# Two kinds of matmuls into one PSUM bank, in alternation or in separate runs

## The chip, the cores and the metric

The kernel runs on one NeuronCore of a Trainium2 chip. The metric is the device time of one execution in microseconds (us), median of several runs. The engines are named as in the profile: PE is TensorE's matmul, PEld its weight load, DVE is VectorE, ACT ScalarE, POOL GpSimd, SP SyncE (here it issues transfers only).

## What is computed

Three blocks follow one another; the change is in the first, a recurrent attention over 768 positions, 4 x 8 heads of 40 elements:

```python
for t in range(S):
    kt, vt, rt = (k[:, :, t], v[:, :, t], r[:, :, t])
    wt, at, bt = (w[:, :, t], a[:, :, t], b[:, :, t])
    y[:, :, t] = np.einsum('bhd,bhde->bhe', rt, state)
    Sa = np.einsum('bhde,bhe->bhd', state, at)
    state_decay = state * wt[:, :, None, :] - np.einsum('bhd,bhe->bhde', Sa, bt)
    state = state_decay + np.einsum('bhd,bhe->bhde', vt, kt)
# then, on x = y with the heads side by side, [4, 768, 320]:
#   u = x + real(fft over positions and features); x = u + relu(norm(u) @ w_ch1) @ w_ch2
#   u = x + token mixing (w_tok1, w_tok2);         x = u + relu(u @ w_ch1) @ w_ch2
```

## The kernel before, in words

**Attention in chunks.** The 768 positions are cut into 12 steps `i` of L=64 positions, each of two halves `c` of H=32. The 32 heads, padded to 33, stand in NG=11 groups `g` of three (3 x 40 = 120 partitions). What the names in the rows mean, in the order of one step: `load` and `decay` bring in and scale the inputs (`bt`, `a`, `R`), `kg` multiplies keys (tile `RT`), `inv` and `merge` make from that a small inverse per head (through `Ge`, `Me`, `Ad` in DRAM, then `AT`, `Mq`, the products mg and mc, tile `Mst`), `kbts` and `pts` transpose (`kbt`, `PT`). Then `chain` carries the state through the two halves: product x (from `L0T` or `L1T`), copied by ScalarE to `X`; product z, copied by ScalarE to `VZt`; product s, added by VectorE into the next half's `L1T` or `L0T`. This is the only part in which a step waits for the step before.

**The outputs of a step: `outp`.** st and zt transpose the state (`SS`, one tile for each half) and `VZt` (`Zd`). For three pairs `k2` of groups of heads, sc multiplies queries (`rm`) with `Zd` and `Vd`, and VectorE masks the result (line 525, tile `sc`). Then y is summed in PSUM from two products for each head, group and half: line 536 multiplies `rm` with the state `SS` (120 rows, 32 columns of the array), line 537 adds the masked `sc` times `kbt` (64 rows from 64c, 32 columns). The result of half c of the x-th group lies on partitions 64x+32c to 64x+32c+31, 40 columns wide; four such quadrants and up to 12 column blocks fill one bank. The groups k=0 to 3 use the bank first, then k=4 and 5; there is one bank for this (`BANKS` has 'y': 1). At the end VectorE multiplies the bank by `PT` into `ys` (line 550; in the last step into `X`, line 543), and that frees the bank.

In step 0 the state before the first half is zero, so line 536 runs only for c=1. That makes 759 products of line 536 and 792 of line 537.

**What sets the order.** Nothing is ordered by hand. Every operation is put into a plan with an engine, a cost, the tiles that it reads and writes and the banks that it takes and frees (`P.op`). `Plan.emit` then walks through a modelled time and gives each engine the ready operation with the earliest latest-start time; `SLACK`, `PW`, `HOLDBACK` and the table `OFF` (a shift for each stage and step) enter into that choice. Where the modelled TensorE has little to do, fillers are laid in (`warm`, 128 x 128 products of the identity). The engines run their lists in that order, whatever the real durations are. The plan charges one y product 0.0275 us (`.33*m` for 12 products of each of m groups).

**After attention.** `begin` frees attention's memory and loads `W1`, `W2` for the first dense block (products hps and acc); the FFT is done with psA and mix; weights are split into high and low parts on VectorE, ScalarE and GpSimd (`job`, tiles `mdraw`, `mdt`, `mda`, `mdh`) beside that.

Of the kernel before, what the change touches and what calls it, by code (L numbers as in the profile page):

```python
# [191 lines left out]
class Attn:  # L192
# [305 lines left out]
    def outp(s,i):  # L498
# [16 lines left out]
        for k2 in range(3):  # L515
            ks=[k for k in (2*k2,2*k2+1)]; gl=[g for k in ks for g in ((k,k+6) if k<5 else (k,))]; m=len(gl); j=(3*i+k2)%NSB; t=s.sc[j]
            hs=s.psum('m',[128,512],"sc"); kc=('ps',hs[0])
            def f(gl=gl,hs=hs):
                ps=s.pst(hs)
                for x,g in enumerate(gl):  # L520
                    for z in range(2):
                        for c in range(2):
                            q=64*c+32*z; nc.tensor.matmul(ps[q:q+32,96*x:96*x+96],lhsT=ZV[z][:,g,H*c:H*c+H],rhs=rm[:,:,g,H*c:H*c+H],start=True,stop=True,skip_group_check=True)  # L523
            P.op('PE',.175*m,f,[('Zd',c) for c in range(2)]+['Vd']+[('rm',p,x) for x in range(3)],[kc,('sc',j)],alloc=hs[0],cols=720*m)
            P.op('DVE',.06+.104*m,lambda t=t,m=m,hs=hs: nc.vector.tensor_tensor(out=t[:,:3*m],in0=s.pst(hs)[:,:96*m].rearrange("p (n t) -> p n t",t=H),in1=s.tri.unsqueeze(1).to_broadcast([128,3*m,H]),op=ALU.mult),[kc,'tri'],[('sc',j)],free=[hs[0]])  # L525
            for k in ks:
                gs=(k,k+6) if k<5 else (k,); m=len(gs)
                if k%4==0:
                    k0=k; hy=s.psum(YB,[128,512],"y"); ky=('ps',hy[0])
                def f(k=k,gs=gs,t=t,hy=hy,k0=k0,gl=gl):  # L530
                    ps=s.pst(hy); c0=120*(k-k0)
                    for hh in range(3):
                        for x,g in enumerate(gs):
# [4 lines left out]
                P.op('PE',.33*m,f,[('rm',p,x) for x in range(3)]+['PT']+[('SS',c) for c in range(0 if i else 1,2)]+[('sc',j),('kbt',i%2)]+([ky+(k0,)] if k>k0 else []),[ky+(k,),('ys',k0)],alloc=hy[0] if k==k0 else None,cols=550*m)
                if i==NSC-1:
                    def mul(u,c,n,hy=hy,k0=k0):  # L540
                        def f(u=u,c=c,n=n,hy=hy,k0=k0):
                            o=s.X[64:128,NSC//2-1].rearrange("p b f -> p (b f)")[:,720*u+c:720*u+c+n]; q=slice(64*u,64*u+64)
                            nc.vector.tensor_tensor(out=o,in0=s.pst(hy)[q,c-120*k0:c-120*k0+n],in1=s.PT[q,c:c+n],op=ALU.mult)
                        P.op('DVE',.06+n*.00106,f,[ky+(y,) for y in range(k0,k+1)]+['PT','close'],[s.xkey(NSC//2-1,('X',i,u,c),720*u+c,n)],free=[hy[0]])
                    if k==2: mul(0,0,360)
                    if k==3: mul(0,360,120); mul(1,0,480)
                    if k==5: mul(0,480,240); mul(1,480,80)
                elif k%4==3 or k==5:
                    def mul(p,c,n,hy=hy,k0=k0):
                        P.op('DVE',.06+n*.00106,lambda: nc.vector.tensor_tensor(out=s.ys[:p,c:c+n],in0=s.pst(hy)[:p,c-120*k0:c-120*k0+n],in1=s.PT[:p,c:c+n],op=ALU.mult),[ky+(y,) for y in range(k0,k+1)]+['PT'],[('ys',k0)],free=[hy[0]])  # L550
                    if k==3: mul(128,0,480)
                    else: mul(128,480,120); mul(64,600,120)
# [98 lines left out]
OFF={'chain': -1.1, 'dec2': 32.2, 'decay': -11.2, 'decode': 1174.5, 'fft': -18.4, 'fft2': -1420.0, 'inv': 0.7, 'kbts': -133.0, 'kg': 2.6, 'load': 73.5,
     'load2': 68.0, 'load3': 495.9, 'loada': 131.7, 'merge': 3.4, 'mlp': 7.2, 'out_tile': -9569.3, 'outp': -0.2, 'pad': 3861.2, 'pts': 110.3,
     'tok': -129.6, 'tok2': -4363.1, 'wdec': 1.9, ('chain', 0): 2.8, ('chain', 1): -0.6, ('chain', 10): -27.7, ('chain', 11): -1181.9,
     ('chain', 2): 2.4, ('chain', 3): 3.1, ('chain', 4): -28.8, ('chain', 5): 1.6, ('chain', 6): 10.0, ('chain', 7): -6253.9, ('chain', 8): -6.2,
     ('chain', 9): -251.5, ('dec2', 0): 39.5, ('decay', 0): -3367.0, ('decay', 1): -9097.8, ('decay', 10): 806.6, ('decay', 11): 4028.4,
     ('decay', 2): -7768.2, ('decay', 3): -4130.3, ('decay', 4): -433.7, ('decay', 5): 3269.8, ('decay', 6): -1157.5, ('decay', 7): 39.5,
     ('decay', 8): -61.1, ('decay', 9): 6.7, ('decode', 0): 1792.1, ('fft', 0): 35.6, ('fft', 1): -29.7, ('fft', 2): -87.9, ('fft', 3): -3601.5,
     ('fft2', 0): 1089.4, ('fft2', 1): -4113.9, ('fft2', 2): -6989.6, ('fft2', 3): 1198.8, ('inv', 0): -4891.5, ('inv', 1): 31.7, ('inv', 2): -3.2,
     ('inv', 3): -25.1, ('inv', 4): -0.6, ('inv', 5): -2644.4, ('inv', 6): -32.2, ('kbts', 0): -5730.2, ('kbts', 1): -4115.9, ('kbts', 10): -4321.1,
     ('kbts', 11): -5664.7, ('kbts', 2): -8815.0, ('kbts', 3): 105.3, ('kbts', 4): -3543.6, ('kbts', 5): 3004.9, ('kbts', 6): -571.5,  # L660
     ('kbts', 7): -4566.8, ('kbts', 8): -1632.3, ('kbts', 9): -4092.9, ('kg', 0): -290.4, ('kg', 1): -112.1, ('kg', 10): -27.7, ('kg', 11): -10105.2,
     ('kg', 2): -1226.0, ('kg', 3): -3903.3, ('kg', 4): -41.2, ('kg', 5): -4.3, ('kg', 6): -8.6, ('kg', 7): 31.3, ('kg', 8): -81.7,
     ('kg', 9): 1517.4, ('load', 0): -9400.7, ('load', 1): -7102.3, ('load', 10): -126.6, ('load', 11): 2473.4, ('load', 2): -251.0,
     ('load', 3): -59.8, ('load', 4): -55.0, ('load', 5): -56.4, ('load', 6): -422.8, ('load', 7): -102.7, ('load', 8): 833.6, ('load', 9): 1196.8,
# [4 lines left out]
     ('loada', 0): -8412.4, ('loada', 1): -306.7, ('loada', 10): 354.9, ('loada', 11): 3605.4, ('loada', 2): -1343.5, ('loada', 3): -2356.9,  # L669
     ('loada', 4): -100.1, ('loada', 5): 2846.4, ('loada', 6): 2227.9, ('loada', 7): 1032.9, ('loada', 8): 2713.4, ('loada', 9): -197.4,  # L670
     ('merge', 0): -4614.6, ('merge', 1): -5007.5, ('merge', 10): 66.6, ('merge', 11): 19.4, ('merge', 2): 1.1, ('merge', 3): -993.9,
     ('merge', 4): 1021.8, ('merge', 5): -653.9, ('merge', 6): -0.8, ('merge', 7): -10626.2, ('merge', 8): 4254.3, ('merge', 9): 46.5,
     ('mlp', 0): -91.8, ('mlp', 1): -0.1, ('mlp', 2): 27.3, ('mlp', 3): 38.4, ('out_tile', None): 5521.2, ('outp', 0): -3.2, ('outp', 1): 5.8,
     ('outp', 10): 2.3, ('outp', 11): -1451.3, ('outp', 2): 0.3, ('outp', 3): -14.1, ('outp', 4): -1.2, ('outp', 5): 2.6, ('outp', 6): -51.3,
     ('outp', 7): -1.8, ('outp', 8): 1.3, ('outp', 9): 57.3, ('pad', 0): -12666.1, ('pts', 0): 1883.5, ('pts', 1): -5413.7, ('pts', 10): -1354.5,
     ('pts', 11): -2249.8, ('pts', 2): -129.1, ('pts', 3): -687.3, ('pts', 4): 1669.8, ('pts', 5): -3554.0, ('pts', 6): -3523.7, ('pts', 7): -115.1,
# [457 lines left out]
```

## Time and profile before

| | us |
|---|---|
| median of 3 runs | 1414.76 (1413.27 to 1424.5) |
| profiled execution | 1415.79 |
| its span, first to last instruction | 1414.1 |
| PE busy | 1358.7 (96%) |
| PEld busy | 1185.6 (84%) |
| DVE busy | 598.8 (42%) |
| ACT busy | 369.9 (26%) |
| POOL busy | 245.0 (17%) |

Busy times are of the whole span. How late a stage begins, at which granted clock TensorE works in it and what it waits for there is read from windows and from the chain of waits. The granted clock is given as a share of 2.4 GHz; it has two levels, 1.00 (2.4 GHz) and 0.50 (1.2 GHz), and a number between them is a mean over time.

### The profile page before, as it was taken

How to read it: one execution, taken by the hardware profiler on the slowest of the kernel's cores; microseconds unless marked ns; L12 is line 12 of the kernel's file. 1: busy time of each engine (PE TensorE's matmuls, PEld its weight loads, DVE VectorE, ACT ScalarE, POOL GpSimd, SP SyncE). 2: the span in 40 equal slices, each digit the busy share in tenths (PEclk: the TensorE clock that was granted, in tenths of full speed). 3: DMA queues.
4: the chain of work that ended last, by engine and by line, in shares of the span. 5: the costliest groups of instructions: out<-in, count | busy, mean ns of one | idle time of the engine just before them, and what ended most of it. 6: DMA issues, size and time to landing. Idle time of an engine off the chain costs nothing.

```text
span 1414.1 us, 36859 instructions
## 1 busy us (share of the span) xinstructions
PE 1358.7 (96%) x16271; PEld 1185.6 (84%) x16271; DVE 598.8 (42%) x1340; ACT 369.9 (26%) x818; POOL 245.0 (17%) x346
## 2 busy tenths in 40 slices
PE   6479999999999999989999999999999999999999
PEld 5467777877777777767877799999999999999998
DVE  5664331435333332110321397877772732323222
ACT  3342131423223222130211142332331411212121
POOL 8530112212120201010011120333442000000000
PEclk9675565666565665555555699999999999999999
DMA  8874222527242231270113231334449000000000
GB/s 180 143 143 108 60 59 44 119 60 150 68 122 70 64 77 47 48 207 16 50 49 103 103 132 62 112 120 138 135 153 335 1 1 15 15 15 15 14 15 28
DMA packets 140478, 120.01 MB, mean 85 GB/s; under 512 B 97983, under 2 KB 117951, under 8 KB 140191
## 3 DMA queue, kind: packets, MB, share of 16 engines
q1 hardware_dynamic: 135519, 94.00, 26.8%
q0 software_dynamic: 4800, 23.67, 4.8%
q8 instruction: 127, 2.08, 0.6%
q14 instruction: 32, 0.26, 0.1%
HBM read 82.26 MB, written 30.61 MB: 80 GB/s over the span
## 4 chain that ended last, share of the span: by engine, by line
PE 88%; DMA 4%; DVE 3%; issue 2%; POOL 1%; ACT 1%; SPq 1%; ACTq 0%; POOLq 0%; DVEq 0%
PE hps L962 17%; PE acc L952 16%; PE y L537 14%; PE y L536 14%; PE s L481 3%; PE sc L523 3%; PE kg L322 2%; PE z L467 2%; PE kbt L429 2%; PE x L460 2%; PE st L505 2%; PE zt L512 2%; PE psA L869 2%; PE mix L896 1%; PE tps L1026 1%
## 5 line engine op out<-in xcount | busy, mean ns | idle before, releaser
L537 PE MATMUL y<-kbt,sc 64*32 64x40 f32 x1584 | 247.3, 258 | 0.0
L536 PE MATMUL y<-SS,rm 120*32 120x40 f32 x1518 | 246.3, 259 | 0.6 <-issue 0.6
L965 DVE SCALAR_TENSOR_TENSOR hl<-hps,hh 128x384 fp32r<-128x384 f32 x176 | 97.9, 557 | 230.2 <-ACT hh L964 230.0
L537 PEld LDWEIGHTS y<-kbt,sc 64*32 64x32 f32 x1584 | 130.7, 132 | 64.1 <-issue 0.8
L536 PEld LDWEIGHTS y<-SS,rm 120*32 120x32 f32 x1518 | 131.5, 133 | 61.5 <-PE warm L54 0.2
L964 ACT ACTIVATE hh<-hps 128x384 fp32r<-128x384 f32 x176 | 86.4, 491 | 328.1 <-PE hps L962 328.1
L962 PE MATMUL hps<-th,v 128*128 128x384 f32 x576 | 142.4, 338 | 0.0
L952 PE MATMUL acc<-v,hh 128*128 128x320 f32 x576 | 129.0, 311 | 0.0
L962 PE MATMUL hps<-th,W 128*128 128x384 f32 x480 | 120.1, 338 | 1.0 <-DVE hl L965 1.0
L952 PE MATMUL acc<-W,hh 128*128 128x320 f32 x480 | 107.6, 311 | 0.0
L962 PEld LDWEIGHTS hps<-th,v 128*128 128x128 f32 x576 | 103.7, 188 | 0.0
L952 PEld LDWEIGHTS acc<-v,hh 128*128 128x128 f32 x576 | 97.9, 188 | 0.0
L550 DVE TENSOR_TENSOR ys<-y,PT 128x480 f32<-128x480 f32 (+2 forms) x33 | 13.0, 403 | 191.4 <-PE y L537 178.4
L57 POOL TENSOR_SCALAR_AFFINE_SELECT RT<-RT 32x384 f32<-32x384 f32 (+1 forms) x66 | 43.7, 670 | 267.7 <-ACT RT L236 265.6
L952 PE MATMUL acc<-v,hl 128*128 128x320 f32 x288 | 89.1, 309 | 0.0
L962 PEld LDWEIGHTS hps<-th,W 128*128 128x128 f32 x480 | 86.8, 188 | 1.4 <-DVE hl L965 1.3
L830 POOL TENSOR_TENSOR mda<-mda,mdh 128x320 f32<-128x320 f32 (+2 forms) x44 | 45.0, 1027 | 208.5 <-ACT mdh L827 94.8
L952 PEld LDWEIGHTS acc<-W,hh 128*128 128x128 f32 x480 | 81.0, 188 | 0.0
L952 PE MATMUL acc<-W,hl 128*128 128x320 f32 x240 | 74.1, 309 | 0.6 <-DVE hl L965 0.6
L525 DVE TENSOR_TENSOR sc<-sc,tri 128x384 f32<-128x384 f32 (+1 forms) x36 | 18.7, 523 | 111.8 <-PE sc L523 111.5
L962 PE MATMUL hps<-tl,v 128*128 128x384 f32 x192 | 64.6, 337 | 0.0
L236 ACT ACTIVATE VZt<-z 32x320 f32<-32x320 f32 x96 | 41.0, 428 | 70.9 <-PE z L467 69.1
(190 smaller groups left out, 2279.7 us busy)
## 6 DMA issues: line engine op xcount, KB each, us to landing
bt<-in_bkR_dram SPq DMA_DIRECT2D x12, 660.0 KB
mdraw<-in_moe_w_ch_dram SPq DMA_DIRECT2D x22, 320.0 KB
wS<-in_wR_dram SPq DMA_DIRECT2D x12, 335.2 KB
a<-in_aR_dram SPq DMA_DIRECT2D x12, 335.2 KB
Vd<-in_vR_dram SPq DMA_DIRECT2D x12, 330.0 KB
VZt<-in_vT_dram SPq DMA_DIRECT2D x24, 165.0 KB
rm<-in_rR_dram SPq DMA_DIRECT2D x36, 110.0 KB
out_dram<-ou SPq DMA_DIRECT2D x24, 160.0 KB
```

What stands on the lines that cost most here:

```text
L57: nc.gpsimd.affine_select(out=o,in_=o,pattern=pattern,compare_op=ALU.is_gt,fill=0.0,base=base,channel_multiplier=-1)
L236: s.P.op('ACT',cost,lambda: s.nc.scalar.activation(out=out,in_=in_() if callable(in_) else in_,func=AF.Copy,**k),R,W,free=free,due=due)
L322: for c in range(2): nc.tensor.matmul(ps[64*c:64*c+64,96*y:96*y+96],lhsT=bt[:,g+y,c].rearrange("p v t -> p (v t)"),rhs=am[:,:,g+y,H*c:H*c+ ...
L481: for v in range(2): n=2*w+v+4*x; nc.tensor.matmul(ps[64*v:64*v+40,x],lhsT=s.kbt[p][64*c:64*c+64,n],rhs=VZt[64*c:64*c+64,n],start=True,sto ...
L523: q=64*c+32*z; nc.tensor.matmul(ps[q:q+32,96*x:96*x+96],lhsT=ZV[z][:,g,H*c:H*c+H],rhs=rm[:,:,g,H*c:H*c+H],start=True,stop=True,skip_group_ ...
L536: if i or c: nc.tensor.matmul(o,lhsT=rm[:,hh,g,H*c:H*c+H],rhs=s.SS[c][:,g],start=True,stop=False,skip_group_check=True)
L537: nc.tensor.matmul(o,lhsT=t[64*c:64*c+64,3*gl.index(g)+hh],rhs=kbt[64*c:64*c+64,3*g+hh],start=i==0 and c==0,stop=True,skip_group_check=True)
L830: P.op('POOL',.07+d*.00237,lambda: nc.gpsimd.tensor_tensor(out=g("da").bitcast(F32),in0=g("da").bitcast(F32),in1=g("dh").bitcast(F32),op=A ...
L952: nc.tensor.matmul(s.pst(acc[x]),lhsT=a[:,sl],rhs=t[w2][w][:,m],start=(m==0 and n==0),stop=(m==MT-1 and n==2))
L962: for n,(l,r) in enumerate(ops): nc.tensor.matmul(ps,lhsT=l,rhs=r,start=n==0,stop=n==7)
L964: s.act(384,lambda: nc.scalar.activation(out=t["hh"][z],in_=s.pst(h),func=AF.Relu),[kp],[('hh',z)],free=[h[0]])
L965: s.dve(.47,lambda: nc.vector.scalar_tensor_tensor(out=t["hl"][z],in0=s.pst(h),scalar=0.0,in1=t["hh"][z].bitcast(F32),op0=ALU.max,op1=ALU. ...
```

## The change

In `outp` the two products are no longer issued one behind the other. For each use of the bank, first all products with the state go in one operation of the plan (line 525 of the changed kernel: all k of the bank, 48 or 18 products, in step 0 24 or 9), ahead of the sc products; then, as each masked `sc` tile is there, the products with `kbt` go in one operation (line 544; 24 or 18). A product carries the clearing flag (`start`) only where its quadrant has not been begun in this use of the bank (`begun`); before, each product of line 536 cleared. The plan charges the same 0.0275 us for a product. The number and the shapes of all products are the same. The multiplications by `PT` are the same in steps 0 to 10; in the last step the first two are one. `SLACK`, `PW`, `HOLDBACK` and `OFF` have other numbers.

```diff
-SLACK=4.21018271644813
+SLACK=2.103090933238401
...
-            for k in ks:
-                gs=(k,k+6) if k<5 else (k,); m=len(gs)
-                if k%4==0:
-                    k0=k; hy=s.psum(YB,[128,512],"y"); ky=('ps',hy[0])
-                def f(k=k,gs=gs,t=t,hy=hy,k0=k0,gl=gl):
-                    ps=s.pst(hy); c0=120*(k-k0)
+        gk=lambda k: (k,k+6) if k<5 else (k,)
+        bank={}
+        for k0,kr in ((0,range(4)),(4,range(4,6))):
+            hy=s.psum(YB,[128,512],"y"); ky=('ps',hy[0]); begun=set(); bank[k0]=(hy,ky,begun); n=sum(len(gk(k)) for k in kr)
+            def f(hy=hy,k0=k0,kr=kr,begun=begun):
+                ps=s.pst(hy)
+                for k in kr:
                     for hh in range(3):
-                        for x,g in enumerate(gs):
+                        for x,g in enumerate(gk(k)):
+                            for c in range(0 if i else 1,2):
+                                q=64*x+H*c; o=120*(k-k0)+40*hh; nc.tensor.matmul(ps[q:q+H,o:o+40],lhsT=rm[:,hh,g,H*c:H*c+H],rhs=s.SS[c][:,g],start=q not in begun,stop=False,skip_group_check=True); begun.add(q)
+            P.op('PE',.165*n,f,[('rm',p,x) for x in range(3)]+[('SS',c) for c in range(0 if i else 1,2)],[ky,('ys',k0)],alloc=hy[0],cols=275*n)
...
-                                q=64*x+H*c; o=ps[q:q+H,c0+40*hh:c0+40*hh+40]
-                                if i or c: nc.tensor.matmul(o,lhsT=rm[:,hh,g,H*c:H*c+H],rhs=s.SS[c][:,g],start=True,stop=False,skip_group_check=True)
-                                nc.tensor.matmul(o,lhsT=t[64*c:64*c+64,3*gl.index(g)+hh],rhs=kbt[64*c:64*c+64,3*g+hh],start=i==0 and c==0,stop=True,skip_group_check=True)
...
+                def f(ks=ks,gl=gl,t=t,hy=hy,k0=k0,begun=begun):
+                    ps=s.pst(hy)
+                    for k in ks:
+                        for hh in range(3):
+                            for x,g in enumerate(gk(k)):
+                                for c in range(2):
+                                    q=64*x+H*c; o=120*(k-k0)+40*hh; nc.tensor.matmul(ps[q:q+H,o:o+40],lhsT=t[64*c:64*c+64,3*gl.index(g)+hh],rhs=kbt[64*c:64*c+64,3*g+hh],start=q not in begun,stop=True,skip_group_check=True); begun.add(q)
+                P.op('PE',.165*m,f,['PT',('sc',j),('kbt',i%2),ky]+([ky+(0,)] if k2==1 else []),[ky+(k2,)],cols=275*m)
...
-PW=2680.8127923252287
-HOLDBACK=63.60602034250026
+PW=7653.7623164983115
+HOLDBACK=0.0
```

TensorE's list of the kernel before, at the start of the y products of step 1 (the names carry tile numbers: SS_155 and SS_156 are the states of the two halves, rm_142 the queries, sc_159 the masked tile):

```order
L523 MATMUL sc<-rm_142,Zd_143 32x96 x2
L523 MATMUL sc<-rm_142,Vd_144 32x96 x2
L481 MATMUL s<-VZt_140,kbt_152 40x40 x16
L536 MATMUL y<-SS_155,rm_142 32x40
L537 MATMUL y<-kbt_153,sc_159 32x40
L536 MATMUL y<-SS_156,rm_142 32x40
L537 MATMUL y<-kbt_153,sc_159 32x40
```

The last four rows repeat through the step: every product with the state is followed by one with `kbt`.

TensorE's list of the changed kernel, in step 2's chain (x, z and s there), behind the first part of step 1's y products:

```order
L467 MATMUL z<-X_145,Mst_146 32x40 x32
L544 MATMUL y<-kbt_153,sc_158 32x40 x24
L512 MATMUL zt<-ident,VZt_140 120x32 x11
L481 MATMUL s<-VZt_140,kbt_152 40x40 x32
L525 MATMUL y<-SS_155,rm_142 32x40
L525 MATMUL y<-SS_156,rm_142 32x40
```

Line 544 stands in a run of 24 between two links of the chain; line 525 begins a run of 18 (one row each, since the two halves read different tiles).

TensorE's list of the changed kernel, in step 0 (where only one half has products with the state) and the chain around it:

```order
L460 MATMUL x<-L1T_138,RT_132 32x40 x32
L505 MATMUL st<-ident,L1T_138 120x40 x11
L467 MATMUL z<-X_145,Mst_146 32x40 x32
L322 MATMUL kg<-am_117,bt_123 64x96 x6
L525 MATMUL y<-SS_156,rm_141 32x40 x24
L481 MATMUL s<-VZt_140,kbt_152 40x40 x32
L512 MATMUL zt<-ident,VZt_140 120x32 x11
```

The run with the state has moved ahead of step 0's sc products, between z and s of the same step, where no y product stood before.

## Rows read from the trace of the kernel before

**Rows 1.** Windows of three stretches: us; busy PE, PEld, DVE, ACT, POOL; PEclk, DMA, GB/s

```profile
0.00:100.00 100.00, 62.57 (x1364) 55.56 (x1364) 59.10 (x101) 41.10 (x77) 63.90 (x111) 0.79 0.84 162
100.00:802.00 702.00, 691.16 (x10966) 527.95 (x10967) 215.68 (x464) 163.14 (x355) 89.09 (x129) 0.58 0.31 77
802.00:1415.00 613.00, 605.02 (x3943) 602.12 (x3941) 324.01 (x777) 165.66 (x386) 92.01 (x106) 1.00 0.25 81
```

**Rows 2.** Window of the long stretch, PE, instructions of the tile y alone

```profile
100.00:802.00 702.00, 390.01 (x3102) 0.58 0.31 77
```

**Rows 3.** The page's cost groups of the two y products

```profile
L537 PE MATMUL y<-kbt,sc 64*32 64x40 f32 x1584 | 247.3, 258 | 0.0
L536 PE MATMUL y<-SS,rm 120*32 120x40 f32 x1518 | 246.3, 259 | 0.6 <-issue 0.6
```

**Rows 4.** Timeline of PE, step 1, clock 0.50: start, us, instructions

```profile
155.56 0.34 PE L536 MATMUL y<-SS,rm 120*32 120x40 f32 x2
155.83 0.34 PE L537 MATMUL y<-kbt,sc 64*32 64x40 f32 x2
```

**Rows 5.** Timeline of PE around 213 us, clock 1.00

```profile
213.02 0.26 PE L536 MATMUL y<-SS,rm 120*32 120x40 f32 x2
213.21 0.26 PE L537 MATMUL y<-kbt,sc 64*32 64x40 f32 x2
```

**Rows 6.** Timeline of PE, step 0, clock 0.50

```profile
102.71 0.35 PE L537 MATMUL y<-kbt,sc 64*32 64x40 f32 x4
102.98 0.34 PE L536 MATMUL y<-SS,rm 120*32 120x40 f32 x2
```

**Rows 7.** The chain of waits at clock 0.50: start, us, what

```profile
110.54 2.29 PE s L481 x64
...
117.48 1.22 PE x L460 x64
...
147.84 1.22 PE z L467 x64
...
298.87 2.86 PE warm L54 x12
```

**Rows 8.** The chain of waits from 256 to 262 us, at the higher clock

```profile
256.11 0.72 PE z L467 x64
...
259.92 1.35 PE s L481 x64
```

**Rows 9.** The page's cost group of the reader of the y bank

```profile
L550 DVE TENSOR_TENSOR ys<-y,PT 128x480 f32<-128x480 f32 (+2 forms) x33 | 13.0, 403 | 191.4 <-PE y L537 178.4
```

**Rows 10.** Windows free of y, first to last of ten, and sum (columns as rows 1)

```profile
70.00:100.00 30.00, 22.91 (x717) 20.31 (x709) 18.48 (x33) 14.46 (x29) 12.59 (x20) 0.84 0.80 165
130.00:155.50 25.50, 25.50 (x546) 21.25 (x546) 14.17 (x25) 9.06 (x19) 5.41 (x8) 0.50 0.44 103
...
250.00:270.00 20.00, 20.00 (x429) 17.39 (x432) 12.31 (x23) 13.84 (x28) 8.95 (x13) 0.70 0.67 155
320.00:330.00 10.00, 9.97 (x193) 8.74 (x195) 6.82 (x15) 5.07 (x12) 2.14 (x2) 0.82 0.85 147
...
690.00:710.00 20.00, 19.87 (x663) 17.24 (x665) 15.83 (x33) 8.61 (x24) 4.34 (x4) 0.52 0.22 66
sum 175.50, PE 162.68 PEld 139.48 DVE 99.11 ACT 80.44 POOL 39.80; mean PE 16.27 PEld 13.95 DVE 9.91 ACT 8.04 POOL 3.98
```

**Rows 11.** The chain of waits, the longest DMA of the merge

```profile
614.83 9.62 DMA Mq<-Me
```

**Rows 12.** The chain of waits from the last y product to the first hps

```profile
801.08 0.28 PE y L537 x2
...
804.70 8.11 DMA W<-m10h
...
835.92 2.82 PE hps L962 x16
```

More of the change, by code (lines that the diff above doesn't have):

```diff
@@ L514, in outp @@
             s.act(.4,s.Zd[:,:,H*c:H*c+H],lambda hz=hz: s.pst(hz)[:120,:H*NG].rearrange("p (g t) -> p g t",t=H),[kz],[('Zd',c)],free=[hz[0]])
[L515 to L525, printed above, removed]
-            for k in ks:
-                gs=(k,k+6) if k<5 else (k,); m=len(gs)
-                if k%4==0:
-                    k0=k; hy=s.psum(YB,[128,512],"y"); ky=('ps',hy[0])
-                def f(k=k,gs=gs,t=t,hy=hy,k0=k0,gl=gl):
-                    ps=s.pst(hy); c0=120*(k-k0)
-                    for hh in range(3):
-                        for x,g in enumerate(gs):
-                            for c in range(2):
-                                q=64*x+H*c; o=ps[q:q+H,c0+40*hh:c0+40*hh+40]
-                                if i or c: nc.tensor.matmul(o,lhsT=rm[:,hh,g,H*c:H*c+H],rhs=s.SS[c][:,g],start=True,stop=False,skip_group_check=True)
-                                nc.tensor.matmul(o,lhsT=t[64*c:64*c+64,3*gl.index(g)+hh],rhs=kbt[64*c:64*c+64,3*g+hh],start=i==0 and c==0,stop=True,skip_group_check=True)
[L538 to L552, printed above, removed]
@@ new lines, in outp, with f, mul @@
+        gk=lambda k: (k,k+6) if k<5 else (k,)
[5 more added lines that the diff above has]
+                for k in kr:
+                    for hh in range(3):
+                        for x,g in enumerate(gk(k)):
+                            for c in range(0 if i else 1,2):
+                                q=64*x+H*c; o=120*(k-k0)+40*hh; nc.tensor.matmul(ps[q:q+H,o:o+40],lhsT=rm[:,hh,g,H*c:H*c+H],rhs=s.SS[c][:,g],start=q not in begun,stop=False,skip_group_check=True); begun.add(q)
+            P.op('PE',.165*n,f,[('rm',p,x) for x in range(3)]+[('SS',c) for c in range(0 if i else 1,2)],[ky,('ys',k0)],alloc=hy[0],cols=275*n)
+            for k2 in ((0,1) if k0==0 else (2,)):
+                ks=(2*k2,2*k2+1); gl=[g for k in ks for g in gk(k)]; m=len(gl); j=(3*i+k2)%NSB; t=s.sc[j]
+                hs=s.psum('m',[128,512],"sc"); kc=('ps',hs[0])
+                def f(gl=gl,hs=hs):
+                    ps=s.pst(hs)
+                    for x,g in enumerate(gl):
+                        for z in range(2):
+                            for c in range(2):
+                                q=64*c+32*z; nc.tensor.matmul(ps[q:q+32,96*x:96*x+96],lhsT=ZV[z][:,g,H*c:H*c+H],rhs=rm[:,:,g,H*c:H*c+H],start=True,stop=True,skip_group_check=True)
+                P.op('PE',.175*m,f,[('Zd',c) for c in range(2)]+['Vd']+[('rm',p,x) for x in range(3)],[kc,('sc',j)],alloc=hs[0],cols=720*m)
+                P.op('DVE',.06+.104*m,lambda t=t,m=m,hs=hs: nc.vector.tensor_tensor(out=t[:,:3*m],in0=s.pst(hs)[:,:96*m].rearrange("p (n t) -> p n t",t=H),in1=s.tri.unsqueeze(1).to_broadcast([128,3*m,H]),op=ALU.mult),[kc,'tri'],[('sc',j)],free=[hs[0]])
+                def f(ks=ks,gl=gl,t=t,hy=hy,k0=k0,begun=begun):
[6 more added lines that the diff above has]
+                P.op('PE',.165*m,f,['PT',('sc',j),('kbt',i%2),ky]+([ky+(0,)] if k2==1 else []),[ky+(k2,)],cols=275*m)
+            rd=[ky+(k2,) for k2 in ((0,1) if k0==0 else (2,))]+['PT']
+            if i==NSC-1:
+                def mul(u,c,n,hy=hy,k0=k0,rd=rd):
+                    def f(u=u,c=c,n=n,hy=hy,k0=k0):
+                        o=s.X[64:128,NSC//2-1].rearrange("p b f -> p (b f)")[:,720*u+c:720*u+c+n]; q=slice(64*u,64*u+64)
+                        nc.vector.tensor_tensor(out=o,in0=s.pst(hy)[q,c-120*k0:c-120*k0+n],in1=s.PT[q,c:c+n],op=ALU.mult)
+                    P.op('DVE',.06+n*.00106,f,rd+['close'],[s.xkey(NSC//2-1,('X',i,u,c),720*u+c,n)],free=[hy[0]])
+                if k0==0: mul(0,0,480); mul(1,0,480)
+                else: mul(0,480,240); mul(1,480,80)
+            else:
+                def mul(p,c,n,hy=hy,k0=k0,rd=rd):
+                    P.op('DVE',.06+n*.00106,lambda: nc.vector.tensor_tensor(out=s.ys[:p,c:c+n],in0=s.pst(hy)[:p,c-120*k0:c-120*k0+n],in1=s.PT[:p,c:c+n],op=ALU.mult),rd,[('ys',k0)],free=[hy[0]])
+                if k0==0: mul(128,0,480)
+                else: mul(128,480,120); mul(64,600,120)
@@ L647 @@
 DD=60
-PW=2680.8127923252287
-HOLDBACK=63.60602034250026
+PW=7653.7623164983115
+HOLDBACK=0.0
 RING=128
[L651 to L664, printed above, removed]
[4 rows of a table removed]
[L669 to L676, printed above, removed]
-     ('pts', 8): 181.0, ('pts', 9): -66.1, ('tok', 0): -5025.5, ('tok', 1): 26.2, ('tok', 2): -3238.5, ('tok', 3): -8655.9, ('tok2', 0): -1545.8,
-     ('tok2', 1): -6681.6, ('tok2', 2): -6326.6, ('tok2', 3): 2095.9, ('wdec', 0): -11.4}
@@ new lines @@
+OFF={'chain': -0.6, 'dec2': 135.9, 'decay': -912.9, 'decode': -748.7, 'fft': -2.8, 'fft2': -2475.1, 'inv': 0.2, 'kbts': 1.2, 'kg': 2.7, 'load': 2.2,
+     'load2': 25.3, 'load3': 117.9, 'loada': 74.1, 'merge': -2.6, 'mlp': -975.6, 'out_tile': 6704.8, 'outp': -0.2, 'pad': 2438.9, 'pts': -0.7,
+     'tok': 3296.0, 'tok2': -2095.0, 'wdec': 10.9, ('chain', 0): -3181.0, ('chain', 1): 0.1, ('chain', 10): -4853.9, ('chain', 11): -878.4,
+     ('chain', 2): 0.0, ('chain', 3): -2187.2, ('chain', 4): -1287.0, ('chain', 5): -377.9, ('chain', 6): 164.5, ('chain', 7): -825.7,
+     ('chain', 8): -2054.7, ('chain', 9): -437.6, ('dec2', 0): -58.4, ('decay', 0): -2656.7, ('decay', 1): -6037.7, ('decay', 10): -5761.7,
+     ('decay', 11): 1184.7, ('decay', 2): -477.5, ('decay', 3): -2820.6, ('decay', 4): 2317.6, ('decay', 5): -3160.1, ('decay', 6): 1322.5,
+     ('decay', 7): -470.3, ('decay', 8): -3522.2, ('decay', 9): 2100.9, ('decode', 0): 155.2, ('fft', 0): -12.4, ('fft', 1): 4.7, ('fft', 2): 5581.6,
+     ('fft', 3): 3465.3, ('fft2', 0): -1003.4, ('fft2', 1): -731.6, ('fft2', 2): -1599.7, ('fft2', 3): -5166.5, ('inv', 0): -1957.5,
+     ('inv', 1): -1457.9, ('inv', 2): -0.7, ('inv', 3): -1063.6, ('inv', 4): -1426.7, ('inv', 5): -450.1, ('inv', 6): 8.7, ('kbts', 0): -2908.6,
+     ('kbts', 1): -4287.2, ('kbts', 10): 0.2, ('kbts', 11): -2553.2, ('kbts', 2): -1.9, ('kbts', 3): 3872.0, ('kbts', 4): -61.6, ('kbts', 5): -94.6,
+     ('kbts', 6): -1586.6, ('kbts', 7): -4505.7, ('kbts', 8): 2856.3, ('kbts', 9): -6085.0, ('kg', 0): -7881.3, ('kg', 1): -4061.0,
+     ('kg', 10): 2217.5, ('kg', 11): 458.7, ('kg', 2): -1394.6, ('kg', 3): -4212.7, ('kg', 4): -840.7, ('kg', 5): 1551.2, ('kg', 6): -2.5,
+     ('kg', 7): -16.1, ('kg', 8): -3071.0, ('kg', 9): 570.6, ('load', 0): -1108.0, ('load', 1): 3756.1, ('load', 10): 10.5, ('load', 11): 3466.7,
+     ('load', 2): -6193.8, ('load', 3): -2789.2, ('load', 4): -2471.7, ('load', 5): 1794.0, ('load', 6): 3366.3, ('load', 7): -679.7,
[4 rows of a table added]
+     ('load3', 8): -93.9, ('load3', 9): -5087.5, ('loada', 0): -7492.1, ('loada', 1): -4683.1, ('loada', 10): -3856.9, ('loada', 11): -5422.2,
+     ('loada', 2): -1454.7, ('loada', 3): 1096.9, ('loada', 4): -954.9, ('loada', 5): -1700.9, ('loada', 6): -77.8, ('loada', 7): 1546.7,
+     ('loada', 8): -2314.2, ('loada', 9): 4165.9, ('merge', 0): -1291.1, ('merge', 1): -7407.9, ('merge', 10): -90.6, ('merge', 11): -57.0,
+     ('merge', 2): 6.0, ('merge', 3): -50.1, ('merge', 4): 3610.9, ('merge', 5): -22.3, ('merge', 6): 0.1, ('merge', 7): -4879.7, ('merge', 8): -7.0,
+     ('merge', 9): -523.7, ('mlp', 0): -2189.2, ('mlp', 1): 1200.1, ('mlp', 2): 2677.5, ('mlp', 3): 766.9, ('out_tile', None): -928.8,
+     ('outp', 0): 2.5, ('outp', 1): -0.7, ('outp', 10): 22.4, ('outp', 11): -9.7, ('outp', 2): 4.6, ('outp', 3): 9.1, ('outp', 4): -9.2,
+     ('outp', 5): 6.4, ('outp', 6): 625.6, ('outp', 7): -656.0, ('outp', 8): -566.3, ('outp', 9): 0.6, ('pad', 0): 1376.7, ('pts', 0): -1985.0,
+     ('pts', 1): -0.7, ('pts', 10): -1019.0, ('pts', 11): -4948.4, ('pts', 2): -3387.5, ('pts', 3): 1083.0, ('pts', 4): -20.7, ('pts', 5): -1500.7,
+     ('pts', 6): 5383.2, ('pts', 7): -3463.2, ('pts', 8): -2499.1, ('pts', 9): -6197.8, ('tok', 0): -4669.9, ('tok', 1): -4483.8,
+     ('tok', 2): -3600.9, ('tok', 3): 4235.0, ('tok2', 0): 965.7, ('tok2', 1): -2565.1, ('tok2', 2): 2585.2, ('tok2', 3): 600.1, ('wdec', 0): -5.3}
```

8 rows, old and new, of the table OFF are left out of this document.

## The prediction

> **What bounds the kernel now.** I read the windows of three stretches first. From 100 to 802 us TensorE is busy 691.16 of 702 us; from 802 on, 605.02 of 613 [rows 1]. So TensorE's time is the kernel's time, but in two different ways: after 802 the granted clock is 1.00 (2.4 GHz), in the long attention stretch it is 0.58, a mix of the two levels with more of the lower one. The same windows cut down to the tile y say where attention's time sits: 390.01 of the 702 us are y products [rows 2]. The cost groups give two kinds in equal shares, 1518 instructions of L536 and 1584 of L537 [rows 3]. An fp32 product that the program's order lists once has two instructions in the trace, so these are 759 and 792 products, 1551 in all, at 390 / 1551 = 0.251 us each.
>
> That is far too much for 40 columns. In the timeline a product of one kind starts 0.27 us after one of the other kind at the lower clock [rows 4] and 0.19 us after it at the higher [rows 5]. In the first step, where half of the L536 products do not exist, two neighbouring L537 products go in one visit (x4) and the visit still takes 0.27 us [rows 6]. So what is paid for is the **change of kind**, not the product: L536 uses 120 rows by 32 columns of the array, L537 64 by 32. Where one kind stays, the chain shows 32 products of x (104 or 128 rows by 32 columns) in 1.22 us, and 32 of z (32 by 32) in 1.22 us: 0.038 us each [rows 7]. At the higher clock 32 of z take 0.72 us, 0.0225 each [rows 8].
>
> **The change part by part.**
>
> 1. *The y products.* Their number and shapes stay (24, 18 or 48 of one kind in a row instead of single ones). Nearest rows: x for the new L525 (all rows of the array, 32 columns, four column places in turn), z for the new L544 (several row places and four column places in turn, all into one bank). That gives 1551 x 0.038 = 59 us at the lower clock, 35 at the higher. I take the z price for L544; the other end is s, 64 rows by 40 columns, 32 products in 2.29 us [rows 7], 0.072 each and 792 x 0.034 = 27 us more.
>
>    A rule stands against that price. What the rows show is that z, whose four row places write one bank, goes as fast as x [rows 7]. The Trainium skill, TensorEngine Tiling (Array Packing), Restrictions and Gotchas, says that different row tiles cannot access the same PSUM bank at once. The new L544 run alternates rows 0 to 63 and 64 to 127 into one bank, so by the rule the two halves would take turns; z does not bear that out. That outcome has the price of s, and is a rival below.
>
>    A second one: the Trainium skill, TensorE: Matmul & The Clock Gate, Part 3 (What overlaps and what doesn't), says that a weight load overlaps running products only where its row group differs. In a run of L525 all row groups are always in use. The x products are in the same position and take 0.038 us with their loads [rows 7], so the trace does not agree; the outcome is the second rival.
>
> 2. *The clearing flag.* It is a bit of the instruction; no row has a price for it. Below: nothing. Above: one change of kind, 0.27 us, for each of 4 quadrants x 24 bank uses, 26 us. I take nothing, since before every first product cleared and no clearing can be told apart from the other y products in [rows 4].
>
> 3. *The bank is held from the first run to the multiplication.* Before it was held from k=0 as well, and in both kernels the reader is one VectorE multiplication per half (33 at 403 ns [rows 9]); the wait in that row is VectorE waiting for y. The cover is other TensorE work between the runs. Without it one hand-over (multiplication and semaphores, about 0.6 us) x 23 = 14 us.
>
> 4. *The new table.* All engines get another order, but the same matmuls stand up to the last y product, except 148 instead of 122 fillers; six of these (12 instructions) took 2.86 us at the lower clock [rows 7], so 26 are 12 us at most, and they are laid where TensorE would stand idle. The startup up to 100 us (loads, decay, inversion of step 0; no y in it) I leave at 100.
>
> 5. *The other work of 100 to 802.* 691.16 - 390.01 = 301 us of TensorE, not shortened by the change itself. What can move it is the clock and the waits that y covered.
>    - Clock. A mean of 0.58 is 16% of the time at the higher level. z gains 1.22 / 0.72 and s 2.29 / 1.35 [rows 7, 8]: 1.7. So 301 us are 253 + 48 x 1.7 = 335 us of work at the lower clock, with y 335 + 59 = 394. In stretches free of y the clock was 0.50 (130 to 155), 0.70, 0.82, 0.52 and 0.84 [rows 10]; ten such stretches together have 0.62. I take 0.65, as the sparse pairs give way to dense runs: 30% at the higher level, 394 / (0.7 + 0.3 x 1.7) = 326 us. Ends: 0.50 (394 us) and 0.84 (267 us).
>    - Waits. y stood ready to fill every hole. Where it did not, from 70 to 100 us, TensorE was busy 22.91 of 30 us, 24% idle, with DMA engines at 0.80; in the other nine stretches 139.77 of 145.50, 4% idle, but there operands had piled up while TensorE was late [rows 10]. I take 12%, nearer to the low end, because the new order has other work between x, z and s; what is late then is the chain X, VZt, L0T/L1T on ScalarE and VectorE, and at times the merge's DMA (9.62 us for Mq [rows 11]). 326 / 0.88 = 370 us.
>
> 6. *The tail.* After the last y product the order has the same matmuls (fillers apart), and about as many decodes of weights stand behind it. From 802 to the first hps run at 836 a weight DMA of 8.11 us and VectorE lie on the path [rows 12], then TensorE runs full at clock 1.00. 1414.1 - 802 = 612.1 us, kept. What could break it: the decodes behind it, if they fell late.
>
> **Sum.** The profiled execution has 1415.79 us, span 1414.1 and 1.7 around it; the median of the runs, 1414.76, is 1.0 below. 100 + 370 + 612.1 + 1.7 = **1084 us**, 23% less than before.
>
> **Rivals.**
> - *Cold:* attention stays at the lower clock, as from 130 to 155 and from 690 to 710 [rows 10]. 394 / 0.88 = 448: 1162 us. For it: dense y-free work did so; against: other such stretches had 0.70 and 0.82.
> - *Warm:* nearly all at the higher clock, and 7% idle: 394 / 1.7 / 0.93 = 249: 963 us; half-way, at 0.84, 267 / 0.93 = 287: 1001.
> - *Waits bared:* 24% idle at 0.65: 326 / 0.76 = 429: 1143 us. For it: DMA work is 0.31 x 702 = 218 us [rows 1] in a stretch half as long, and VectorE has 216 us there; against: neither fills 370.
> - *Row places take turns in L544:* 27 / 1.21 / 0.88 = 25 more: 1109 us.
> - *Weight loads of L525 not overlapped:* 0.27 us per product remains for 759 of them: 759 x 0.232 / 0.88 = 200 more: 1284 us. Against it stands x.
> - *No change:* the 0.27 us come from something else that a run keeps (40 columns into one bank): 1415 us. Against: [rows 6], x and z.
> - *Slower:* the one y bank. If each of its 23 hand-overs stopped TensorE's queue, y's saving of 390 - 59 = 331 us would be gone at 331 / 23 = 14.4 us each; at 16 us it would be 37 us slower, 1452. Against: the reader is a 0.4 us multiplication [rows 9], and other work is placed between the runs.
>
> **How the numbers follow.** Forecast 1084: 0.55, its own range 1030 to 1130. Cold 0.13, warm 0.13, waits bared 0.10, row places 0.04, weight loads 0.02, no change 0.02, slower 0.01. The range 1000 to 1162 takes in the two clock ends at the idle shares used there; outside lie half of cold, half of warm and the last three, 0.18. About 1% is what a measurement can tell from no change: faster 0.97, within 1% 0.02, slower 0.01.
>
> **What would show it.** Right: y groups together near 50 to 60 us and a timeline with runs of 24 at 0.038 us or less per product; the last y product near 470 us; from it to the end 612 us; the attention stretch's clock near 0.65 and TensorE idle for about 45 us. If y is short but the last product comes at 520 or later, the idle share and the clock tell waits from cold. If L544 alone has 0.07 us a product, row places take turns; if L525 has 0.27, loads do not overlap. The forecast is wrong above all if the tail lengthens because decodes that attention's length had covered now stand before it.

## The result

The changed kernel takes 1123.68 us (median of 4 runs, 1108.95 to 1128.34) against 1415.3 us: a ratio of 0.7895 with a 95% interval of 0.7809 to 0.7981, 21% faster. The ratio is that of the means of the fast runs; the run of 1128.34 us was in a slower state of the chip and is left out of it. Forecast were 1084 us in a range of 1000 to 1162.

| | before | after |
|---|---|---|
| span of the profiled execution, us | 1414.1 | 1122.0 |
| PE busy | 1358.7 (96%) | 1011.3 (90%) |
| DVE busy | 598.8 (42%) | 591.2 (53%) |
| last y product ends, us | 802 | 513 |
| from there to the end, us | 612 | 609 |

Windows of the changed kernel, cut at the end of its last y product (us; busy PE, PEld, DVE, ACT, POOL; PEclk, DMA share, GB/s); the first and the third answer to [rows 1]:

```profile
0.00:100.00 100.00, 70.59 (x1235) 63.15 (x1236) 60.61 (x97) 41.84 (x76) 68.77 (x113) 0.71 0.78 158
100.00:513.10 413.10, 337.00 (x11144) 293.35 (x11143) 216.06 (x470) 161.53 (x355) 92.03 (x125) 0.70 0.54 130
513.10:1122.00 608.90, 603.73 (x3938) 601.66 (x3934) 314.51 (x772) 165.78 (x387) 93.62 (x108) 1.00 0.25 83
```

The same stretch for the tile y alone, which answers to [rows 2]:

```profile
100.00:513.10 413.10, 55.56 (x3054) 0.70 0.54 130
```

y went from 390.0 to 55.6 us of TensorE (24 of the 1551 products now run before 100 us). The rest of TensorE's work in the stretch is 337.0 - 55.6 = 281.4 us (301 before). But TensorE is idle for 413.1 - 337.0 = 76.1 us, against 11 before. The timeline of PE shows both, the dense runs and the new idle time (start, us, instructions, in brackets the idle time ahead):

```profile
186.50 0.51 PE L544 MATMUL y<-kbt,sc 64*32 64x40 f32 x33
187.46 0.34 PE L544 MATMUL y<-kbt,sc 64*32 64x40 f32 x15 [0.45 <-issue]
...
208.35 1.28 PE L467 MATMUL z<-X,Mst 32*32 32x40 f32 x61 [4.89 <-issue]
209.57 1.41 PE L525 MATMUL y<-SS,rm 120*32 120x40 f32 x67
215.00 0.75 PE L525 MATMUL y<-SS,rm 120*32 120x40 f32 x29 [4.03 <-issue]
```

33 instructions of L544 (two to a product) take 0.51 us at the higher clock, where one visit took 0.19 in [rows 5]. The holes stand in the middle of a run, between two products of the same kind, where nothing new is read or waited for.

### The profile page after: what moved, and what is told of

Read it like the earlier page. It is cut to its first block, busy times and chain, and to the rows that moved or that the text cites. A ratio compares the mean times of both kernels' runs of the same rounds, so it can differ in the third digit from the quotient of the medians.

```text
span 1122.0 us, 36924 instructions
## 1 busy us (share of the span) xinstructions
PE 1011.3 (90%) x16311; PEld 958.2 (85%) x16311; DVE 591.2 (53%) x1339; ACT 369.2 (33%) x818; POOL 254.4 (23%) x346
## 4 chain that ended last, share of the span: by engine, by line
PE 81%; issue 7%; POOL 4%; DVE 3%; DMA 2%; ACT 2%; SPq 2%; DVEq 0%; POOLq 0%; ACTq 0%
PE hps L969 22%; PE acc L959 21%; PE s L481 3%; PE sc L535 3%; PE psA L876 3%; PE y L544 2%; PE mix L903 2%; PE y L525 2%; PE kg L322 2%; PE z L467 2%; PE x L460 2%; PE t2ps L1046 2%; PE tps L1033 2%; PE zt L512 2%; PE st L505 2%
## 5 line engine op out<-in xcount | busy, mean ns | idle before, releaser
L57 POOL TENSOR_SCALAR_AFFINE_SELECT RT<-RT 32x384 f32<-32x384 f32 (+1 forms) x66 | 48.6, 745 | 122.7 <-ACT RT L236 107.2
L54 PE MATMUL warm<-ident 128*128 128x128 f32 x348 | 55.2, 307 | 4.0 <-POOL ident masks.py:199 2.0
L959 PEld LDWEIGHTS acc<-v,hl 128*128 128x128 f32 x288 | 54.1, 188 | 0.0
L481 PE MATMUL s<-VZt,kbt 64*40 64x40 f32 x1472 | 47.7, 238 | 7.1 <-issue 7.1
L969 PE MATMUL hps<-tl,W 128*128 128x384 f32 x160 | 54.0, 337 | 0.0
L481 PEld LDWEIGHTS s<-VZt,kbt 64*40 64x40 f32 x1472 | 42.8, 151 | 13.0 <-issue 10.9
L54 PEld LDWEIGHTS warm<-ident 128*128 128x128 f32 x348 | 48.4, 214 | 5.9 <-issue 2.4
```

What stands on the lines that cost most here:

```text
L54: for x in range(m): nc.tensor.matmul(t[:,128*(x%4):128*(x%4)+128],lhsT=ident,rhs=ident,start=True,stop=True)
L57: nc.gpsimd.affine_select(out=o,in_=o,pattern=pattern,compare_op=ALU.is_gt,fill=0.0,base=base,channel_multiplier=-1)
L481: for v in range(2): n=2*w+v+4*x; nc.tensor.matmul(ps[64*v:64*v+40,x],lhsT=s.kbt[p][64*c:64*c+64,n],rhs=VZt[64*c:64*c+64,n],start=True,sto ...
L959: nc.tensor.matmul(s.pst(acc[x]),lhsT=a[:,sl],rhs=t[w2][w][:,m],start=(m==0 and n==0),stop=(m==MT-1 and n==2))
L969: for n,(l,r) in enumerate(ops): nc.tensor.matmul(ps,lhsT=l,rhs=r,start=n==0,stop=n==7)
```

## Experiments

**Undoing the runs: singly, and in fours.** Both kernels issue the products with the state in the operation of the products with `kbt` and have the same order around them; they differ only in how many products of one kind stand together.

```diff
-# in the operation ahead of sc: all products with the state (S)
-# behind each sc tile: all products with kbt (K)
+# e1, behind each sc tile, for every hh, x and c:        S, K
+# e2, behind each sc tile, for every hh:   S for all x and c, then K for all x and c
```

> The changed kernel with its new table and one bank use as it is, but the two kinds of y products alternate again, each product with the state right ahead of its product with kbt. Theory K (what costs is the change of kind): the y group goes back from 56 to about 390 us of TensorE; of the 334 us more some 65 are given back, since y then covers holes again: 1390 us (1350 to 1440). Rival T (the new table made the gain): 1200 us or less.

Measured: 1466.3 us (ratio to before 1.0349, 1.0297 to 1.0401).

> The same plan as the kernel that alternates singly, but in fours: four products with the state (four quadrants), then the four with kbt. Theory K: a quarter of the changes, about 390 x 0.19 to 0.27 = 75 to 105 us for y instead of 56: 1140 to 1180 us. Rival B (what costs is that a product adds to what another has just written into the same bank): the pairs still meet in the bank with the same columns, so little is won against single alternation: over 1300 us.

Measured: 1171.98 us (0.8247, 0.8192 to 0.8302). Windows of the tile y alone, 100 us to the last y product, of e1:

```profile
100.00:838.50 738.50, 394.37 (x3102) 0.58 0.30 74
```

and of e2:

```profile
100.00:548.40 448.40, 110.08 (x3102) 0.68 0.49 120
```

e1 has about 1520 visits of one kind, e2 12 x 36 = 432. That is 394.37 / 1520 = 0.26 us and 110.08 / 432 = 0.255 us a visit, at mean clocks of 0.58 and 0.68: the price hangs on the visit, not on what stands in it (one product or four). The theory of the changing kind holds, and the table is not what won. Rival B is not settled by e2 alone, since four products now lie between two that meet in the bank; the stretches in two banks below (e8) settle it. e1 came out above its range: y is as dear as expected (339 us more than in the changed kernel), but it gave back 39 us of idle time instead of 65, the other work took 307 instead of 281 us at the lower clock (0.58), and the tail was 11 us longer. The two windows of e1, to its last y product and behind it:

```profile
100.00:838.50 738.50, 701.83 (x11104) 536.01 (x11104) 215.19 (x475) 162.43 (x356) 89.55 (x127) 0.58 0.30 74
838.50:1458.40 619.90, 610.91 (x3969) 607.17 (x3968) 315.24 (x767) 165.94 (x386) 93.20 (x106) 0.99 0.24 80
```

With single alternation the new plan and table are thus slower than the kernel before.

**The clearing flag.**

```diff
-start=q not in begun
+start=True            # every product with the state
```

> The changed kernel, but every product with the state carries the clearing flag; the sums in PSUM are then not the wanted ones (earlier state products are overwritten). If clearing is free, as the prediction took it: 1124 us within 1%. If each clearing costs a change of kind (0.19 to 0.27 us): 759 - 92 more of them, 125 to 180 us more.

Measured: 1125.27 us (0.7953, 0.7912 to 0.7995), the changed kernel's time. Clearing has no price of its own that shows. That only the first product of a quadrant clears keeps the sums right when the two kinds stand in separate runs; it is not what makes them fast.

**The old table under the runs.**

```diff
-SLACK=2.103090933238401   # and PW, HOLDBACK, OFF
+SLACK=4.21018271644813    # the numbers of the kernel before
```

> The separate runs with the old numbers of SLACK, PW, HOLDBACK and OFF. Theory K: the runs alone bring most of it, 1124 us plus up to 80 (the old table was not made for this structure). Rival T (the table made the gain): over 1350 us.

Measured: 1131.26 us (0.7991, 0.7953 to 0.8030). The runs alone bring 98% of the gain. Against e3 on the same chip, which has the changed kernel's order, the new table is worth 6 us; the intervals overlap, so even that is not settled.

**Whose is the idle time? Fewer and more products with the state.**

```diff
 # e5: the operation of the products with the state issues nothing
-nc.tensor.matmul(ps[q:q+H,o:o+40],lhsT=rm[...],rhs=s.SS[c][:,g],start=q not in begun,stop=False,...)
 # e7: it issues each twice
+nc.tensor.matmul(ps[q:q+H,o:o+40],lhsT=rm[...],rhs=s.SS[c][:,g],start=False,stop=False,...)
```

> The changed kernel without the products with the state: 759 products are left out (1518 matmul and 1518 weight-load instructions), everything else stands in the same order. TensorE stood idle for 76 us between 100 and 513 us in the changed kernel. Theory F (idle because TensorE's code is loaded in blocks, here one every 128 matmuls): 12 of 87 blocks fewer, so 27 us less busy time and 8 to 14 us less idle time: 1083 to 1093 us. Theory W (idle because ScalarE, VectorE or DMA are late): the chain is no shorter, the idle time grows by most of the 27 us: 1110 to 1124 us.

Measured: 1088.15 us (0.7658, 0.7635 to 0.7680).

> The changed kernel with every product with the state issued twice (the sums then hold it doubled): 12 blocks of code more. Theory F: 27 us more busy time and 8 to 14 us more idle time: 1155 to 1170 us. Theory W: much of the added work goes into the holes: 1124 to 1140 us.

Measured: 1167.62 us (0.8225, 0.8192 to 0.8257). The windows from 100 us to the last y product, of e5:

```profile
100.00:472.80 372.80, 310.96 (x9626) 268.81 (x9618) 217.84 (x458) 160.43 (x349) 92.28 (x125) 0.70 0.57 139
```

and of e7:

```profile
100.00:554.80 454.80, 362.31 (x12594) 317.89 (x12584) 214.67 (x470) 161.65 (x355) 86.24 (x125) 0.71 0.49 119
```

Idle are 61.8 us in e5, 76.1 in the changed kernel, 92.5 in e7: more TensorE work makes more idle time, 14.3 and 16.4 us for 12 blocks each, somewhat more than the 8 to 14 expected. Had TensorE waited for other engines, work put into the queue would have filled the holes. Both times lie in the range of the theory of code loading and outside the other's. The waits put down to "issue" (time in which the engine waited for nothing that the profile shows) say it more sharply: 49 us in e5, 73 in the changed kernel, 87 in e7. In e5 TensorE's waits for other engines and DMA rose as well, from 3 to 13 us, so theory W has a small part there, and the 14.3 us are some 24 less of the one and some 10 more of the other. The page's queue for instructions has 12 packets fewer in e5 and 12 more in e7 than the 128 of the changed kernel (packets, MB, share):

```profile
q8 instruction: 116, 1.90, 0.8%
q8 instruction: 140, 2.29, 0.8%
```

**Without fillers.**

```diff
-FILL=(0.22,5749.5)
+FILL=(0.0,5749.5)
```

> The changed kernel without the 174 fillers. Theory F: 2.7 blocks of code fewer and 10 to 15 us of fillers less on TensorE: 1105 to 1120 us if the clock stays at 0.70 in attention. If the fillers hold the clock up, it falls towards 0.6 and the time rises to 1130 to 1150 us.

Measured: 1140.53 us (0.8030, 0.8005 to 0.8056), the upper expectation in time, but not where it was expected. Windows of e6, cut at its last y product:

```profile
100.00:511.10 411.10, 333.45 (x10871) 287.16 (x10868) 223.68 (x478) 166.37 (x359) 94.88 (x131) 0.67 0.53 133
511.10:1138.60 627.50, 607.03 (x3880) 601.97 (x3880) 314.05 (x760) 165.67 (x384) 90.73 (x102) 0.98 0.23 78
```

Attention is 2 us shorter without fillers (clock 0.67 instead of 0.70); the loss is behind it, 627.5 instead of 608.9 us. There TensorE's waits are 17 us against 1.7 in the changed kernel, nearly all for VectorE (the longest, 3.9 us, for the tile `tl`), and it is busy 3 us longer. So VectorE's work falls later against TensorE's in this run. The order is not the same in all places; whether the missing fillers or the changed order do that stays open.

**The price of a change by itself.** Eight stretches of 192 products of the identity stand behind the changed kernel's end:

```diff
+for n in range(192): mm(at_(ta,n), 0, 120)                       # (1) 120 rows x 32 columns
+for n in range(192): mm(at_(ta,n), 64*(n%2), 64*(n%2)+64)        # (2) 64 x 32
...
+    else: mm(at_(tb,n//2+2), 64*(n//2%2), 64*(n//2%2)+64)        # (4) (1) and (2) in turn, two banks
...
+for n in range(192): mm(at_(ta,0), 0, 120)                       # (8) always the same quadrant
```

> The changed kernel with eight stretches of 192 small products behind its end, nothing else running: (1) 120 rows x 32 columns alone, (2) 64 x 32 alone, (3) both in alternation in one bank, (4) both in alternation in two banks, (5) 120 and 104 rows in alternation, (6) 64 x 32 and 32 x 32 in alternation, (7) 120 x 32 and 120 x 64 in alternation, (8) 120 x 32 always on the same quadrant. Theory K: 0.02 to 0.04 us a product in 1, 2, 5 and 0.19 to 0.27 in 3, 4, 6, 7. Rival B (the shared bank): 4 is as cheap as 1. Theory F: in 1, 2 and 5 a hole of 1 to 2 us every 128 matmul instructions although no other transfer runs, and none in 3 and 4, whose 128 matmuls last long enough.

Windows of e8 inside stretches 3, 4, 6 and 7 (the first still holds the last products of stretch 2):

```profile
1139.00:1190.00 51.00, 51.00 (x390) 33.94 (x380) 0.00 (x0) 0.00 (x0) 0.00 (x0) 0.50 0.00 1
1191.00:1242.00 51.00, 51.00 (x379) 34.01 (x378) 0.00 (x0) 0.00 (x0) 0.00 (x0) 0.50 0.00 1
1252.00:1302.00 50.00, 50.00 (x377) 33.00 (x376) 0.00 (x0) 0.00 (x0) 0.00 (x0) 0.50 0.00 1
1303.00:1363.00 60.00, 60.00 (x377) 44.30 (x376) 0.00 (x0) 0.00 (x0) 0.00 (x0) 0.50 0.00 1
```

Two instructions are a product: 51.00 us for 379 of them in stretch 4 are 0.27 us a product, the price of [rows 4], with no other engine at work, in two banks and in two different quadrants; stretch 3, in one bank and one quadrant for each pair, is the same. No product adds to another here, so rival B falls. In the same way 64 and 32 rows in turn (6) cost 50.00 / 188.5 = 0.27, 32 and 64 columns (7) 60.00 / 188.5 = 0.32. e8 was run once. The timeline of stretches 1 and 2 (and the start of 3), with the first full block of stretch 5 as last row:

```profile
1119.80 1.78 PE L1120 MATMUL probe<-ident 120*32 120x40 f32 x177
1123.77 1.62 PE L1120 MATMUL probe<-ident 120*32 120x40 f32 x128 [2.18 <-issue]
1127.24 2.62 PE L1120 MATMUL probe<-ident 120*32 120x40 f32 x128 [1.85 <-issue]
1130.71 2.35 PE L1120 MATMUL probe<-ident 64*32 64x40 f32 x128 [0.85 <-issue]
1134.73 2.35 PE L1120 MATMUL probe<-ident 64*32 64x40 f32 x128 [1.67 <-issue]
...
1246.95 1.63 PE L1120 MATMUL probe<-ident 120*32 120x40 f32 x128 [0.57 <-issue]
```

There the products alone take 0.02 to 0.04 us (stretch 1 mostly at the higher clock, stretch 2 at the lower), and after every 128 matmul instructions TensorE stands for 0.57 to 2.18 us. In stretches 3, 4, 6 and 7 there is no such hole. In stretch 5 (120 and 104 rows in turn) a product takes 0.03 us, so that change costs nothing. Stretch 8, always on one quadrant:

```profile
1364.00:1379.00 15.00, 15.00 (x380) 14.96 (x378) 0.00 (x0) 0.00 (x0) 0.00 (x0) 0.90 0.02 3
```

That is 0.08 us a product: using one quadrant over and over costs something without any change of kind, but far less than 0.27. There is no hole either, though 128 matmuls last only some 5 us there.

## Why the prediction was right, and where it was short

**The main step held.** What is paid for is the change of kind: e1 and e2 price the visit at 0.26 us whatever is in it, e8 shows the change by itself with other data and separate banks. The Trainium skill, TensorEngine Tiling (Array Packing), Key Properties, says that changing the tiling mode drains TensorE. Stretches 3, 4, 6 and 7 agree that such a change costs time and give the price at the lower clock: 0.27 us for rows (120 and 64, 64 and 32) and 0.32 for columns.

**The price of the runs.** 49 us were forecast for y (59 / 1.21), 55.6 measured. In the chain, 48 products of L525 took 1.76 us at the lower clock, 0.037 each, and 47 took 1.02 us at the higher, 0.022: the prices of x and z in [rows 7, 8].

```profile
151.17 1.02 PE y L525 x94
...
435.19 1.76 PE y L525 x96
```

So neither rival of the runs came: weight loads of L525 overlap, and L544 is no dearer (2.35 us for 64 products of its shape in stretch 2 of e8, 0.037 each at the lower clock). The rule of the Trainium skill that the prediction set against this price, that different row tiles cannot access one bank at once (TensorEngine Tiling (Array Packing), Restrictions and Gotchas), shows no price here, as z had let expect.

**The clearing flag** at nothing: right (e3). **The bank held longer** at nothing: right; VectorE's multiplications ended 0.8 us of TensorE's waits at L525. (The 403 ns of [rows 9] are a mean over three sizes; the longest takes 0.66 us, and that was still hidden.) **The tail** at 612: 609. **The new table** at nothing beyond the other work: within 6 us (e4).

**The clock.** 0.65 was taken, 0.70 came. That did not shorten the other work as it should have: 277 us forecast, 281.4 measured. By the sum's own factor 281.4 us at 0.70 are 360 us of work at the lower clock, not 335. The 26 fillers more are 12 of these 25 at most; the rest stays open.

**The step that was mis-sized is the idle share**: 12%, 44 us, forecast; 18.4%, 76.1 us, measured. With y 7 us and the other work 4 us over, that is the 43 us by which attention is longer than forecast (413 for 370); 3 come back in the tail. The time lies inside the forecast's own range (1030 to 1130), near its upper end, and not by luck of errors that cancel: nearly all go one way. The reason given was wrong as well. The prediction named the chain of `X`, `VZt`, `L0T`/`L1T` on ScalarE and VectorE and the merge's DMA. The waits of TensorE from 100 to 513 us (engine, line, who ended the wait: us in total, times, longest) say otherwise:

```profile
PE z L467 <- issue: 14.2, 8, 4.9
PE mc L417 <- issue: 12.3, 7, 2.5
PE y L525 <- issue: 10.2, 6, 4.0
PE y L544 <- issue: 8.7, 8, 1.9
PE x L460 <- issue: 7.7, 5, 3.5
PE sc L535 <- issue: 6.6, 4, 2.5
PE s L481 <- issue: 6.1, 5, 1.8
...
PE mc L417 <- ACT T L236: 1.0, 1, 1.0
```

"issue" makes up 73 of the 76 us. Windows of the changed kernel between the end of one hole and the begin of the next, at four places (the second column is the length, the third PE's busy time and count):

```profile
105.56:108.60 3.04, 3.00 (x128) 2.61 (x128) 1.75 (x8) 0.00 (x0) 0.00 (x0) 0.50 1.04 223
110.93:114.55 3.62, 3.56 (x128) 2.69 (x128) 3.52 (x7) 1.71 (x4) 1.89 (x2) 0.50 0.75 130
122.60:125.10 2.50, 2.44 (x128) 2.20 (x127) 2.40 (x6) 0.65 (x2) 0.00 (x0) 0.50 0.02 7
207.50:211.00 3.50, 2.62 (x128) 2.37 (x127) 0.00 (x0) 1.27 (x3) 0.00 (x0) 0.50 0.93 172
```

At all four it is 128 matmuls and 128 weight loads (one of them may fall out of a window's edge), 256 instructions. The page's DMA part has a queue for instructions (packets, MB, share):

```profile
q8 instruction: 128, 2.10, 0.8%
```

2.10 MB / 128 = 16 KB a packet; the page's 16311 matmuls and 16311 weight loads, in blocks of 256, are 127 blocks, about as many as packets. TensorE's program comes in such blocks. While 256 instructions lasted some 17 us (128 x 0.135 us in [rows 4]), a block was there in time; in a run they last 2.5 to 3.6 us, and TensorE waits. The times of the packets in the trace say the same: each of the 53 waits put down to "issue" in this stretch ends 1.2 to 2.0 us after a packet of this queue has landed, each of the seven in e8 1.3 to 1.6 us after. The Trainium skill, Runtime: NRT & Kernel Launch, Instruction fetch mechanics, gives the same block of 16 KiB or 256 instructions and calls the crossing mostly hidden. The size agrees; the hiding does not hold for runs of small matmuls: 73 us over 11144 x 2 / 256 = 87 blocks are 0.84 us for each here, and 0.57 to 2.18 us at the end of e8, where hardly any other transfer runs (DMA share 0.02 in stretch 2). Shown are the spacing (after, e8), the landing of a packet ahead of each hole's end, and that holes come and go with instructions (e5, e7). That busy DMA engines lengthen a hole is likely (the longest, 4.89 us, ended at 208, with the DMA share at 1), but was not tried apart.

So the price of a product in a run has a second term beside its time in the array, four instructions of code, and the row that showed it was in the trace of before: of TensorE's 12 us of waits from 100 to 802 us, 10.8 were "issue", 9.4 of them at mc and mg, runs of small matmuls (columns as above):

```profile
PE mc L417 <- issue: 7.3, 3, 3.0
PE mg L408 <- issue: 2.1, 3, 1.1
```

How large the second term gets can be estimated from stretches 1 and 2 of e8: there work begins again at 1123.77, 1127.24, 1130.71 and 1134.73 us, so a block takes 3.5 to 4.0 us whether its matmuls need 1.6 us or 2.4 to 2.6. For its 64 products that is 0.054 to 0.063 us each, more than the 0.038 of the sum.

Of the rivals, "waits bared" (24% idle, 1143 us) was nearest to what happened, with 18.4%, though for another reason than it gave; "row places take turns" (1109 us) is nearer in time, but its sign, 0.07 us a product in L544 alone, did not come.

## What to carry to other kernels

Keep matmuls of one array shape together (120 and 104 rows counted as one shape here, 64 and 32 as others): a change of shape cost about 0.27 us at the lower clock whatever stood between two changes, and a timeline in which a 40-column product takes as long as the change shows it. Once small matmuls run densely, count instructions as well as columns: idle time put down to "issue" in the middle of a run, every 256 instructions, was TensorE's own code coming in here; fewer instructions made less of it (e5), and where 256 instructions lasted 5 us or more with hardly any other transfer (e8) it did not show. A plan that charges 0.0275 us for a product is right only if the emitted order keeps the shapes together.

## What the hardware showed that was not expected

- Code loading stops TensorE for 0.57 to 2.18 us every 256 instructions in a run of small fp32 matmuls, with no other engine at work (e8); in attention it is 73 us of 413.
- 120 and 104 rows in turn cost nothing (0.03 us a product), 120 and 64 cost 0.27 in one bank or in two, 64 and 32 cost 0.27 and a change of column width 0.32 (both tried in one bank).
- Clearing the bank with every product costs nothing (1125.27 us against 1123.68).
- Leaving the fillers out costs 17 us, and not in attention, where the clock was lowest, but in the tail (627.5 us against 608.9), where TensorE then waits for VectorE.
